# A key tile's split, a modulation row's low part and a layer norm's statistics moved in an adaLN block with linear attention

## The chip, the cores and the metric

The kernel runs on one core of a Trainium2 chip. The metric is the device time of one execution in microseconds (us). TensorE (PE) multiplies, with its weight loads (PEld) overlapping the matmuls; VectorE (DVE), ScalarE (ACT) and GpSimd (POOL) do the elementwise work; the queue of SyncE (SP) issues all the transfers. Each engine runs its instructions strictly in the order in which the program lists them, so moving a line moves work on every engine that it uses.

## The reference

For x of 2048 tokens by 512 features, six rows of 512 come out of `silu(c) @ w_mod`: sa, ca, ga, sb, cb, gb.

```python
h = layernorm(x) * (1 + ca) + sa
q, k, v = split_heads(h @ wqkv)                 # 32 heads of 16
pq, pk = phi(q), phi(k)                         # phi(t) = (t+1 if t>0 else exp(t)) + 1e-6
kv, z = sum_s pk^T v, sum_s pk
x = x + ga * (((pq @ kv) / (pq . z + 1e-6)) @ wo)
h = layernorm(x) * (1 + cb) + sb
x = x + gb * (((h @ w_gate) * (h @ w_up)) @ w_down)   # F = 1376
```

All of it is float32. The kernel keeps this precision in the large products by splitting each operand into a rounded high part and a low part, `a = ah + al`, and adding three products: `ah bh + ah bl + al bh`.

## The kernel before

The 2048 tokens are four chunks of four tiles of 128 tokens. Tile `i` is tile `j = i % 4` of chunk `ch = i // 4`. All working tiles of 128 x 512 take their buffers from one pool of 94, in the order in which the program asks for them; PSUM has four accumulator banks (`acc`) and four working banks (`bank`).

**Splits.** `split(src, h, l)` is one ScalarE copy (L194, the high part) and one subtraction on VectorE (L195, the low part), or on GpSimd where `low=nc.gpsimd` is given. `split_raw` takes two fresh buffers and splits a loaded weight or a row. `k_split_x(i)` does the same for key tile i: it splits the normalised tile `norm[ch].n[j]` into xh and xl (L194/L195, or L386/L387 for chunks 2 and 3). `k_split(i)` splits phi(k) into kh and kl (L405/L406).

**The key loop (L565 to L656)**, one iteration for each of the 16 tiles. Iteration i projects key tile i+2 (`proj(i + 2, wk)`), in some iterations a query tile too, prepares the splits of tile i+1 (`k_split_x`, `k_split`), runs phi on the projected tile (`k_phi`, L372, L373 and L376), adds to z (L399) and accumulates x^T phi(k) of tile i on TensorE (`t_tile`, L414 to L416). In between, the next chunks' layer norms are prepared. In iteration j = 2 of chunks 0 and 1 `nx2.stats` and `rstd_of` (GpSimd's power, L263) start the norm of the chunk after the next. In iteration j = 3 (i = 3 for chunk 2, i = 7 for chunk 3) it goes on:

- i = 3: the shift of tiles 0 and 1 (`nmr_of(0, 2)`, VectorE, L267), their normalised tiles (`xhat_blocks`, ScalarE, L279), their transfers out to DRAM (`lift_out`, SP), and only then `k_split_x(4)` and `k_split(4)`. Tiles 2 and 3 follow further down in the same iteration, with transfers back (`lift_in`, L332, four for each tile).
- i = 7: tiles 0 and 1 with their transfers out, the shift of tiles 2 and 3 (`nmr_of(2, 4)`), these tiles and their transfers out, the sixteen transfers back, and then `k_split_x(8)` and `k_split(8)`.

The transfers turn a tile blockwise; `lift_turn` (VectorE, L336) finishes the turn, `lift_row` (ScalarE, L341) applies the modulation, and `lift_parts` (L349, L351, L352) splits the result. These parts are the left operands of the chunk's projections: those of chunk 2 are wanted first by `proj(8, wk)` in iteration 6, those of chunk 3 by `proj(12, wk)` in iteration 10.

`extra` is a table of work that the loop does at the end of certain iterations; its entries 3, 5, 6 and 7 split the four loaded blocks of the value weight into `wv`. `wv` is used after the loop.

**After the loop (L771 to L817)**, in the order of the program: queries 6 and 7; the split of `accs[5]` (the row gb before its sum over partitions) and, through `mod_row` (L183, L189), its row; the products that make the key-value matrix in the bank `kvps` (L788), masked by L796; denominators of chunk 0, each a product of phi(q) with z (`den_p`, L676) and a sum over a head's 16 features (`den_r`, L682), then an addition and a reciprocal for the chunk (`den_b`, L692 and L693); `den_c(i)` (L700) divides a query tile, `ready(i)` divides it and sends it out (`move_out`), `move_in(i)` fetches it back turned. `w_out(a, b)` multiplies the key-value blocks of groups a and b by the output weight, each product in a bank of its own, read out by VectorE with the row ga (L765), and then splits both. `q_b(i)` is the last step of phi on a query tile (L376) and frees the bank of its projection.

**The attention output (L1275 to L1298).** `turn_a(i)` transposes a query tile on TensorE into a bank (L714); `y_a` is the product that gives the output tile (L838), `y_b` reads it out on ScalarE with the two sums that the second layer norm wants (L250, L251). `norm2[0].rstd_of()` makes the variance of chunk 0 (L260, VectorE) and takes the power on GpSimd (L263); `ln2_nx(0)` is `nmr_of` (L267) and the four normalised tiles (`ln2_xhat`, L272, ScalarE); `ln2_turn` transposes them (L293).

Of the kernel before, what the change touches and what calls it, by code (L numbers as in the profile page):

```python
# [24 lines left out]
def tile_adaln_block(  # L25
# [12 lines left out]
    nc = tc.nc  # L38
# [6 lines left out]
    NCH = S // CH  # L45
# [87 lines left out]
    raw_v = load_qkv(2)  # L133
# [59 lines left out]
    def split(src, h, l, low=None):  # L193
        nc.scalar.activation(h, src, AF.Copy)  # L194
        (low or nc.vector).tensor_tensor(l, src, f32(h), op=ALU.subtract)  # L195

    def split_raw(raw, shape=(P, D), low=None):
        h = B("w", shape, F32R)
        l = B("w", shape, F32R)
        split(raw, h[:raw.shape[0]], l[:raw.shape[0]], low)  # L200
        return h, l
# [158 lines left out]
    def proj(i, w, of=bank):  # L360

        ch, j = divmod(i, NJ)
        ps = of()
        rows = w is wq and i not in FLIPPED
        product(ps.rearrange("p (s q i) -> p s q i", q=NQ, i=BL) if rows else ps,
                [(cut(norm[ch].t[k], j * P, (j + 1) * P), tuple(by_row(x) for x in w[k]) if rows else w[k])
                 for k in range(KD)])
        return ps
# [9 lines left out]
    def k_split_x(i):  # L378
        ch, j = divmod(i, NJ)
        kx[i] = [B("xh", dt=F32R), B("xl", dt=F32R)]  # L380
        if ch not in LIFTED:
            split(norm[ch].n[j], *kx[i])
            return
        x = by_row(norm[ch].n[j])
        h, l = (t.rearrange("p (s q i) -> p s q i", q=NQ, i=BL) for t in kx[i])
        nc.scalar.activation(h, x, AF.Copy)  # L386
        nc.vector.tensor_tensor(l, x, f32(h), op=ALU.subtract)  # L387
# [30 lines left out]
    def q_a(i, ps):  # L418
        phq[i] = B("h")
        q_ps[i] = ps  # L420
        phi_a(ps, phq[i])

    def q_b(i):
        phi_b(q_ps.pop(i), phq[i])
# [113 lines left out]
    accs = {}  # L538
# [6 lines left out]
    def mod_part(v, *ks):  # L545
        if 0 in ks:
            accs[v] = B("f")
        mod_acc(accs[v], raw_m[v], ks)

    extra = {3: lambda: (wv.extend(split_raw(r) for r in raw_v[0:1]),),  # L550
             5: lambda: (wv.extend(split_raw(r) for r in raw_v[1:2]),),
             6: lambda: (wv.extend(split_raw(r) for r in raw_v[2:3]), mod_load(2),),
             7: lambda: (wv.extend(split_raw(r) for r in raw_v[3:4]),),
             8: lambda: (mod_part(2, 0, 1), mod_load(3)),
# [10 lines left out]
    for i in range(NT):  # L565
        ch, j = divmod(i, NJ)
        done = 0
        up = ch + 1 if 0 < ch < NCH - 1 else None
        if i in (6, 10):
            qps = proj(q_at[i], wq)  # L570
        if i > 2 and i != NT - 2:
            ahead[i + 2] = proj(i + 2, wk) if i + 2 < NT else proj(i + 6 - NT, wq)
        if i in q_at and i not in (6, 10):
            qps = proj(q_at[i], wq)
        def turn_x():
            to, *ks = turn_at[i]
            nx.transpose(*ks)
            nx.modulated(ca, sa, *ks, cast=nc.vector)
            norm[to:] = [nx]

        if i == 2:
            turn_x()
            wq.extend(split_blocks(r) for r in raw_q)
        if ch + 2 < NCH and j == 3:
            nx = nx2
            if ch == 0:
                nx.nmr_of(0, 2)
            nx.xhat_blocks(0, 1)
            lifts = [lift_out(f"first_{ch}_{n}", nx.n[n]) for n in range(2)]
            if ch:  # L590
                nx.nmr_of(2, 4)
                nx.xhat_blocks(2, 3)
                lifts += [lift_out(f"first_{ch}_{n}", nx.n[n]) for n in (2, 3)]
                lifts = [lift_in(x) for x in lifts]
        if 0 < i < NT - 1:
            k_split_x(i + 1)
            k_split(i + 1)
        if up and j == 1:
            if up == 2:
                lift_turn(2, lifts[2])  # L600
                lift_turn(3, lifts[3])
            for k in range(KD):
                nx.t[k] = lift_parts(k, lift_row(k, ca, sa))
            norm[up:] = [nx]
        if i in turn_at and i != 2:
            t_tile(i, 0, 1)
            done = 2
            turn_x()
        if i == 2:
            t_tile(i, *range(KD))  # L610
            done = KD
            ahead[i + 2] = proj(i + 2, wk)
        if ch + 2 < NCH and j == 2:
            nx2 = Norm(xts[ch + 2])
            nx2.stats(0, 1)
            nx2.rstd_of(0, 2)
            if ch:
                nx2.stats(2, 3)
                nx2.nmr_of(0, 2)
                nx2.rstd_of(2, 4)  # L620
        if ch == 0 and j == 3:
            nx.stats(2, 3)
            nx.rstd_of(2, 4)
        if i + 2 < NT:
            k_phi(i + 2, ahead.pop(i + 2))
        elif i == NT - 1:
            q_a(i + 6 - NT, ahead.pop(i + 2))
            q_b(i + 6 - NT)
        if i in q_at:
            q_a(q_at[i], qps)  # L630
            q_b(q_at[i])
        if ch == 0 and j == 3:
            nx.nmr_of(2, 4)
            nx.xhat_blocks(2, 3)
            lifts[0], lifts[1] = lift_in(lifts[0]), lift_in(lifts[1])
            lifts += [lift_out(f"first_{ch}_{n}", nx.n[n]) for n in (2, 3)]
            lifts[2], lifts[3] = lift_in(lifts[2]), lift_in(lifts[3])
        if i + 1 < NT:
            z_add(i + 1)
        if i == NT - 2:  # L640
            pairs["z"] = split_raw(zacc, low=nc.gpsimd)
        if i == NT - 1:
            zps = row_sum(pairs["z"])
            zb = consts.tile([P, D], F32, name="zb")
            nc.scalar.activation(zb, zps, AF.Identity, bias=eps_z)
            zq = B("z")
            nc.gpsimd.tensor_copy(zq.rearrange("p (q s i) -> p q s i", q=NQ, i=BL), by_block(zb))
        t_tile(i, *range(done, KD))
        if up == 2 and j == 0 or ch == 1 and j == 3:
            lift_turn(0, lifts[0])  # L650
            lift_turn(1, lifts[1])
        if up == 3 and j == 0:
            lift_turn(2, lifts[2])
            lift_turn(3, lifts[3])
        if i in extra:
            extra[i]()  # L656
# [16 lines left out]
    def den_p(ch, *js, on=None):  # L673
        for j in js:
            pzs[ch, j] = B("f")
            (on or nc.gpsimd).tensor_tensor(pzs[ch, j], phq[ch * NJ + j], zq if ch * NJ + j in FLIPPED else zb, op=ALU.mult)  # L676
# [7 lines left out]
    def den_a(ch, *js, on=None):  # L684

        for j in js:
            den_p(ch, j, on=on)
            den_r(ch, j)

    def den_b(ch, a=0, b=NJ):  # L690
        d = dens[ch][:, a:b]
        nc.vector.tensor_tensor(d, d, (den0q if ch * NJ + a in FLIPPED else den0).unsqueeze(1).to_broadcast([P, b - a, NH]), op=ALU.add)  # L692
        nc.vector.reciprocal(d, d)  # L693

    def den_c(*tiles):

        for i in tiles:
            ch, j = divmod(i, NJ)
            p3 = phq[i].rearrange("p (h i) -> p h i", i=DH)
            nc.vector.scalar_tensor_tensor(p3, p3, EPS_PHI, dens[ch][:, j].unsqueeze(2).to_broadcast([P, NH, DH]),  # L700
                                           op0=ALU.add, op1=ALU.mult)
# [35 lines left out]
    def move_in(*tiles):  # L737

        for i in tiles:
            moved[i] = lift_in(moved[i])  # L740
# [12 lines left out]
    def ready(*tiles):  # L753
        den_c(*tiles)
        move_out(*tiles)
# [3 lines left out]
    def w_out(*gs):  # L759
        fs = []  # L760
        for g in gs:
            ps = bank()
            product(ps, [(cut(kvp, g * P, (g + 1) * P), wo_s[g])])
            f = B("n")
            nc.vector.tensor_tensor(f, ps, ga, op=ALU.mult)  # L765
            fs.append(f)
        for f in fs:
            wp.append((B("w", dt=F32R), B("w", dt=F32R)))
            split(f, *wp[-1])
# [9 lines left out]
    for f in fs:  # L779
        tt.append((B("w", dt=F32R), B("w", dt=F32R)))  # L780
        split(f, *tt[-1])
    q_a(6, ps)
    q_tile(7)
    pairs[5] = split_raw(accs[5], low=nc.gpsimd)
    kvps = bank()
    for g in range(KD):
        a, b = g * P, (g + 1) * P
# [16 lines left out]
    q_a(8, ps)  # L804
    ps = proj(9, wq)
    q_b(8)
    w_out(0, 1)
    q_a(9, ps)
    den_c(0)
    ready(2)  # L810
    move_in(2)
    w_out(2, 3)
    ready(3)
    den_c(1)
    move_in(3)
    q_b(9)
    q_tile(10)  # L817


# [132 lines left out]
    def ln2_xhat(ch):  # L952
        norm2[ch].xhat(0, 1, 2, 3)

    def ln2_nx(ch):
        norm2[ch].nmr_of()
        ln2_xhat(ch)
# [328 lines left out]
    y_step(2, lambda: split_gu(f0, nc.gpsimd))  # L1286
    den_a(1, 1, on=nc.vector)
    y_step(3, lambda: scale_down(f0), turn=False, seed=False)
    den_a(1, 2, 3, on=nc.vector)
    den_b(1)  # L1290
    ps12 = proj(12, wq)
    y_b(3)
    norm2[0].rstd_of()
    ready(4)
    q_a(12, ps12)
    ps13 = proj(13, wq)
    ready(5)
    ln2_nx(0)  # L1298
    q_b(12)
    ready(6)  # L1300
    move_in(4)
# [227 lines left out]
```

## Time and profile before

| | |
|---|---|
| median of 3 runs | 550.17 us (549.89 to 550.17) |
| the profiled execution | 550.99 us, of it 549.3 us from the first to the last instruction |
| mean granted TensorE clock | 0.996 |
| PE busy | 542.7 us (99%) |
| PEld busy | 444.3 us (81%) |
| DVE, ACT, POOL busy | 382.7, 293.1 and 206.4 us |

Times in the profile count from the first instruction of the profiled execution. A row of the timeline reads: start, duration, engine, line of the kernel, operation, output tile and input tiles, output and input shape, count, and in brackets the engine's idle time just before it with what ended that. Engines are pipelined: the next independent instruction may start some 0.1 us before the last one's end. A name like `h` stands for all tiles of that name.

### The profile page before, as it was taken

How to read it: one execution, taken by the hardware profiler on the slowest of the kernel's cores; microseconds unless marked ns; L12 is line 12 of the kernel's file. 1: busy time of each engine (PE TensorE's matmuls, PEld its weight loads, DVE VectorE, ACT ScalarE, POOL GpSimd, SP SyncE). 2: the span in 40 equal slices, each digit the busy share in tenths (PEclk: the TensorE clock that was granted, in tenths of full speed). 3: DMA queues.
4: the chain of work that ended last, by engine and by line, in shares of the span. 5: the costliest groups of instructions: out<-in, count | busy, mean ns of one | idle time of the engine just before them, and what ended most of it. 6: DMA issues, size and time to landing. Idle time of an engine off the chain costs nothing.

```text
span 549.3 us, 7400 instructions
## 1 busy us (share of the span) xinstructions
PE 542.7 (99%) x2432; PEld 444.3 (81%) x2432; DVE 382.7 (70%) x631; ACT 293.1 (53%) x541; POOL 206.4 (38%) x208
## 2 busy tenths in 40 slices
PE   8999999999999999999999999999999999999997
PEld 6888778888878878878888888877888888888886
DVE  6897789989988888769766676985444344434434
ACT  3595777747477774577674545444443444444110
POOL 2001010001003320066696566766666646446100
PEclk9899999999999999999999999999999999999999
DMA  8902426220074245945454061790444122200004
GB/s 281 384 24 78 153 83 216 89 74 2 20 211 143 93 169 159 304 142 152 133 144 124 23 208 39 254 288 16 121 135 114 57 58 58 58 19 1 0 1 154
DMA packets 68455, 65.65 MB, mean 120 GB/s; under 512 B 8448, under 2 KB 46592, under 8 KB 68416
## 3 DMA queue, kind: packets, MB, share of 16 engines
q1 hardware_dynamic: 68416, 65.17, 37.9%
q8 instruction: 19, 0.31, 0.2%
q14 instruction: 20, 0.16, 0.1%
HBM read 46.27 MB, written 18.87 MB: 119 GB/s over the span
## 4 chain that ended last, share of the span: by engine, by line
PE 94%; DVE 2%; ACT 1%; DMA 1%; SPq 1%; issue 0%; POOL 0%; DVEq 0%; POOLq 0%
PE bank L1097 33%; PE acc L1177 6%; PE acc L1178 6%; PE acc L1179 6%; PE acc L838 5%; PE bank L209 5%; PE bank L207 5%; PE bank L208 4%; PE acc L416 3%; PE acc L414 3%; PE acc L415 3%; PE bank L921 2%; PE bank L923 2%; PE bank L922 2%; PE acc L948 1%; PE acc L947 1%
## 5 line engine op out<-in xcount | busy, mean ns | idle before, releaser
L1097 PE MATMUL bank<-h,w 128*128 128x512 f32 (+1 forms) x798 | 184.7, 390 | 0.0
L1097 PEld LDWEIGHTS bank<-h,w 128*128 128x128 f32 (+1 forms) x798 | 148.5, 186 | 33.2 <-ACT bank L1102 0.6
L1102 ACT ACTIVATE bank<-bank 128x512 f32<-128x512 f32 (+1 forms) x38 | 22.2, 583 | 139.5 <-PE bank L1097 139.4
L908 DVE TENSOR_TENSOR x<-acc,x 128x512 f32<-128x512 f32 (+1 forms) x73 | 48.8, 682 | 49.6 <-PE acc L1179 47.9
L1083 POOL TENSOR_TENSOR w<-raw,w 128x256 fp32r<-128x256 f32 (+3 forms) x38 | 40.8, 1073 | 91.2 <-ACT w L1076 91.2
L1177 PE MATMUL acc<-w,kh 128*128 128x512 f32 (+2 forms) x154 | 59.7, 387 | 0.0
L1178 PE MATMUL acc<-w,kh 128*128 128x512 f32 (+2 forms) x154 | 59.6, 387 | 0.0
L1179 PE MATMUL acc<-w,kl 128*128 128x512 f32 (+2 forms) x154 | 59.6, 387 | 0.0
L195 POOL TENSOR_TENSOR w<-raw,w 128x512 fp32r<-128x512 f32 (+1 forms) x26 | 36.7, 1415 | 56.4 <-ACT w L194 52.2
L263 POOL TENSOR_TENSOR rstd<-ve,half 128x2 f32<-128x2 f32 (+3 forms) x13 | 12.6, 970 | 113.0 <-DVE ve L262 67.4
L1083 POOL TENSOR_TENSOR w<-t,w 128x512 fp32r<-128x512 f32 (+1 forms) x38 | 49.2, 1314 | 0.0
L195 DVE TENSOR_TENSOR kl<-u,kh 128x512 fp32r<-128x512 f32 (+1 forms) x38 | 26.4, 735 | 30.6 <-ACT kh L194 30.6
L207 PE MATMUL bank<-w,h 128*128 128x512 f32 x104 | 40.9, 394 | 0.0
L209 PE MATMUL bank<-w,h 128*128 128x512 f32 x104 | 40.9, 393 | 0.0
L208 PE MATMUL bank<-w,h 128*128 128x512 f32 x104 | 40.6, 390 | 0.0
L838 PE MATMUL acc<-w,xh 128*128 128x512 f32 x120 | 37.1, 391 | 0.0
L1156 DVE TENSOR_TENSOR u<-bank,u 128x512 f32<-128x512 f32 (+1 forms) x19 | 13.1, 691 | 31.4 <-PE bank L1097 23.8
L1177 PEld LDWEIGHTS acc<-w,kh 128*128 128x128 f32 (+1 forms) x154 | 28.9, 188 | 6.0
L1179 PEld LDWEIGHTS acc<-w,kl 128*128 128x128 f32 (+1 forms) x154 | 28.9, 188 | 5.9
L1178 PEld LDWEIGHTS acc<-w,kh 128*128 128x128 f32 (+1 forms) x154 | 29.0, 188 | 5.9
L1065 POOL TENSOR_TENSOR t<-raw,t 128x256 f32<-128x256 f32 (+1 forms) x34 | 25.8, 760 | 1.3
L838 PEld LDWEIGHTS acc<-w,xh 128*128 128x128 f32 x120 | 22.5, 188 | 4.6
(215 smaller groups left out, 1114.1 us busy)
## 6 DMA issues: line engine op xcount, KB each, us to landing
raw<-in_w_mod_dram SPq DMA_DIRECT2D x24, 256.0 KB, 3.6
raw<-in_B_w_down_dram SPq DMA_DIRECT2D x20, 256.0 KB, 2.8
raw<-in_B_w_gate_dram SPq DMA_DIRECT2D x36, 128.0 KB, 3.3
raw<-in_B_w_up_dram SPq DMA_DIRECT2D x36, 128.0 KB, 3.5
x<-in_A_x_dram SPq DMA_DIRECT2D x16, 256.0 KB, 5.5
out_dram<-x SPq DMA_DIRECT2D x15, 256.0 KB, 2.7
moved<-h SPq DMA_DIRECT2D x14, 256.0 KB, 2.1
u<-moved SPq DMA_DIRECT2D x56, 64.0 KB, 2.0
```

The costliest lines, as they stand in the source:

```text
L195: (low or nc.vector).tensor_tensor(l, src, f32(h), op=ALU.subtract)
L207: nc.tensor.matmul(ps, ah, bh, start=i == 0, stop=False)
L208: nc.tensor.matmul(ps, ah, bl, start=False, stop=False)
L209: nc.tensor.matmul(ps, al, bh, start=False, stop=i == n - 1)
L838: nc.tensor.matmul(yps[i], x, y, start=False, stop=k == KD - 1 and x is al, skip_group_check=True)
L908: nc.vector.tensor_tensor(xt[:, a:b], dn[j][:, a:b], xt[:, a:b], op=ALU.add)
L1065: sub = lambda out, x, y: (on or nc.gpsimd).tensor_tensor(out, x, y, op=ALU.subtract)
L1083: sub = lambda out, x, y: (on or nc.gpsimd).tensor_tensor(out, x, f32(y), op=ALU.subtract)
L1097: mm = lambda x, y, **kw: nc.tensor.matmul(ps, x[:, k], y, skip_group_check=True, **kw)
L1177: nc.tensor.matmul(ps, hh[:, a:b], dh[:n, c:d], start=i == 0, stop=False)
L1178: nc.tensor.matmul(ps, hh[:, a:b], dl[:n, c:d], start=False, stop=False)
L1179: nc.tensor.matmul(ps, hl[:, a:b], dh[:n, c:d], start=False, stop=i == len(hs) - 1)
```

## The change

Three groups of lines move; nothing else is added or removed.

1. In the key loop at j = 3 of chunks 0 and 1, `k_split_x(i + 1)` comes ahead of the next normalised tiles (at i = 3 after the shift of tiles 0 and 1, at i = 7 ahead of everything of this block). At i = 3 the split of the first block of the value weight comes right behind it and leaves the table `extra`.
2. After the loop the split of `accs[5]` goes ahead of `q_a(6)`, with its low part on VectorE instead of GpSimd; the divisions of tiles 0 and 2 and tile 2's transfers go ahead of `w_out(0, 1)`; `den_c(1)` and `q_b(9)` go ahead of `ready(3)`.
3. In the attention output, `rstd_of` of the second norm goes ahead of the last sum of chunk 1's denominators and their addition and reciprocal, `nmr_of` right behind these, and the normalised tiles right behind `q_a(12)`.

```diff
-    extra = {3: lambda: (wv.extend(split_raw(r) for r in raw_v[0:1]),),
-             5: lambda: (wv.extend(split_raw(r) for r in raw_v[1:2]),),
+    extra = {5: lambda: (wv.extend(split_raw(r) for r in raw_v[1:2]),),
...
             nx = nx2
             if ch == 0:
                 nx.nmr_of(0, 2)
+            k_split_x(i + 1)
+            if ch == 0:
+                wv.append(split_raw(raw_v[0]))
             nx.xhat_blocks(0, 1)
...
         if 0 < i < NT - 1:
-            k_split_x(i + 1)
+            if ch + 2 == NCH or j < 3:
+                k_split_x(i + 1)
             k_split(i + 1)
...
+    pairs[5] = split_raw(accs[5])
     q_a(6, ps)
     q_tile(7)
-    pairs[5] = split_raw(accs[5], low=nc.gpsimd)
...
     q_b(8)
-    w_out(0, 1)
-    q_a(9, ps)
     den_c(0)
     ready(2)
     move_in(2)
+    w_out(0, 1)
+    q_a(9, ps)
     w_out(2, 3)
+    den_c(1)
+    q_b(9)
     ready(3)
-    den_c(1)
     move_in(3)
-    q_b(9)
     q_tile(10)
...
-    den_a(1, 2, 3, on=nc.vector)
-    den_b(1)
+    den_a(1, 2, on=nc.vector)
+    den_p(1, 3, on=nc.vector)
     ps12 = proj(12, wq)
     y_b(3)
     norm2[0].rstd_of()
+    den_r(1, 3)
+    den_b(1)
+    norm2[0].nmr_of()
     ready(4)
     q_a(12, ps12)
+    ln2_xhat(0)
     ps13 = proj(13, wq)
     ready(5)
-    ln2_nx(0)
     q_b(12)
```

## The prediction

> **What bounds the kernel now.** I read the chain of waits first, then the waits of the weight loads, then the timeline around each edit. The chain:
>
> ```profile
> PE 94%; DVE 2%; ACT 1%; DMA 1%; SPq 1%; issue 0%; POOL 0%; DVEq 0%; POOLq 0%
> ```
>
> TensorE is the bound nearly throughout, so an edit can pay only where TensorE stops. Its stops show as waits of its weight loads (microseconds in total, times, longest):
>
> ```profile
> PEld bank L209 <- DVE h L352: 1.0, 3, 0.4
> PEld bank L714 <- DVE h L376: 0.7, 1, 0.7
> ...
> PEld bank L293 <- ACT n L272: 0.6, 1, 0.6
> ```
>
> Row 1 is the key projection of tile 8, which waits for the second chunk's turned tiles (the split at L352); row 2 is the turning of tile 1 (L714); the last is the second layer norm of chunk 0. The edits lie ahead of these three places, and all that can be won is some 2.5 us of 549.3.
>
> **The first edit, at tile 3.** ScalarE idles ahead of the normalised tiles, then does the split of key tile 4 (xh) behind them; the split of the value weight (w) comes an iteration later:
>
> ```profile
> 47.23 1.52 ACT L279 ACTIVATE n<-x,nmr,rstd 128x512 f32<-128x512 f32 x2 [3.97 <-DVE nmr L267]
> 48.66 0.62 ACT L194 ACTIVATE xh<-n 128x512 fp32r<-128x512 f32 x1
> ...
> 55.16 0.61 ACT L194 ACTIVATE w<-raw 128x512 fp32r<-128x512 f32 x1
> 55.68 0.62 ACT L194 ACTIVATE xh<-n 128x512 fp32r<-128x512 f32 x1
> ...
> 64.17 0.81 ACT L341 ACTIVATE f<-wide,col,col 128x512 f32<-128x512 f32 x1 [3.83 <-DVE wide L336]
> ```
>
> Both instructions move into the idle 3.97 us, where they cost nothing; left of the chain, each frees 0.52 us (55.16 to 55.68), 1.04 together. Their VectorE halves (0.61 each, from the two starts below) fall into VectorE's own gap, since at this place the norm's shift (nmr) stays ahead of them:
>
> ```profile
> 49.31 0.69 DVE L195 TENSOR_TENSOR xl<-n,xh 128x512 fp32r<-128x512 f32 x1 [2.11 <-ACT xh L194]
> 49.92 0.69 DVE L406 SCALAR_TENSOR_TENSOR kl<-phi,kh 128x512 fp32r<-128x512 f32 x1
> ...
> 59.24 0.69 DVE L376 SCALAR_TENSOR_TENSOR h<-bank,h 128x512 f32<-128x512 f32 x1 [0.46 <-ACT h L373]
> ```
>
> At 59.24 VectorE waits for ScalarE, and from there on it is busy without a gap up to the row at 64.17; so the turned rows and their splits come 1.04 earlier. The transfers of tiles 2 and 3 on SP's queue follow their tiles, about 0.5 earlier, and still land before VectorE wants them. What TensorE loses there:
>
> ```profile
> 63.80 0.39 PE L207 MATMUL bank<-w,h 128*128 128x512 f32 x1
> ...
> 66.52 0.39 PE L207 MATMUL bank<-w,h 128*128 128x512 f32 x1
> ...
> 70.02 0.39 PE L414 MATMUL acc<-kh,xh 128*128 128x512 f32 x1
> ```
>
> Twelve matmuls take 2.72 us unhindered and 3.50 in tile 8's projection: 0.78 lost, all of it covered by 1.04. **Gain 0.78**; between 0 (if something else of that chain does not move) and 0.78.
>
> **The same edit at tile 7.** Here the split of key tile 8 goes ahead of the shift for tiles 2 and 3 as well, on VectorE's queue:
>
> ```profile
> 77.44 0.68 DVE L399 TENSOR_TENSOR z<-z,phi 128x512 f32<-128x512 f32 x1
> ...
> 80.91 0.69 DVE L387 TENSOR_TENSOR xl<-n,xh 128x512 fp32r<-128x512 f32 x1 [2.11 <-ACT xh L386]
> ...
> 86.05 0.71 DVE L336 STREAM_TRANSPOSE wide<-u 128x512 f32<-128x512 f32 x1 [0.32 <-DMA u<-first]
> ...
> 96.03 0.69 DVE L352 TENSOR_TENSOR h<-f,h 128x512 fp32r<-128x512 f32 x1
> ```
> ```profile
> 78.84 1.52 ACT L279 ACTIVATE n<-x,nmr,rstd 128x512 f32<-128x512 f32 x2 [1.10 <-DVE nmr L267]
> ```
>
> Queued behind the 0.60 of xl are the shift, ScalarE's two tiles at 78.84, their two transfers out on SP and, behind them on SP, all sixteen transfers back. The turn at 86.05 waits for one of those; from it to the last split at 96.03 VectorE has no gap. All this comes 0.60 later by its own clock. TensorE loads that split with next to no slack (96.72 is its end):
>
> ```profile
> 96.80 0.19 PEld L209 LDWEIGHTS bank<-w,h 128*128 128x128 f32 x1
> ```
>
> But VectorE arrives 1.04 earlier and TensorE only 0.78, so of the 0.60 some 0.26 is absorbed and 0.08 is slack: the load is about 0.3 late. A late load costs less than its lateness, since loads run one matmul ahead (0.23): about 0.12 less. **Loss 0.18**; bounds 0 and 0.40 (if nothing is absorbed).
>
> **The row's low part.** GpSimd's subtraction goes to VectorE, into the wait of 0.93 in the first row here (it needs 0.60). It is gone from beside the denominator product of the second row, which took 1.79 next to it; operations of this size take 0.69:
>
> ```profile
> 134.24 0.69 DVE L376 SCALAR_TENSOR_TENSOR h<-bank,h 128x512 f32<-128x512 f32 x1 [0.93 <-ACT h L373]
> 134.85 1.79 DVE L676 TENSOR_TENSOR f<-h,zb 128x512 f32<-128x512 f32 x1
> ...
> 144.92 1.37 DVE L765 TENSOR_TENSOR n<-bank,row 128x512 f32<-128x512 f32 x2 [0.40 <-PE bank L209]
> 146.31 1.38 DVE L195 TENSOR_TENSOR w<-n,w 128x512 fp32r<-128x512 f32 x2
> 147.60 1.29 DVE L700 SCALAR_TENSOR_TENSOR h<-h,den 128x512 f32<-128x512 f32 x2
> 148.80 1.28 DVE L765 TENSOR_TENSOR n<-bank,row 128x512 f32<-128x512 f32 x2
> ```
>
> VectorE gains 1.1 us there but then waits for the key-value product and for ScalarE's copy behind the modulation row: **0**, bounds 0 and 0.4 (the idle at 144.92).
>
> **The new order of the output weights.** The two divisions (L700) go ahead of the first two output-weight products. Without them the products of groups 2 and 3 leave PSUM 0.5 earlier than 148.80, and q_b(9) runs before the third division. What TensorE loses to these two now:
>
> ```profile
> 149.25 0.39 PE L209 MATMUL bank<-w,h 128*128 128x512 f32 x1
> 149.54 0.65 PE L714 MATMUL bank<-ident,h 128*128 128x128 f32 x4
> 150.14 0.50 PE L207 MATMUL bank<-w,h 128*128 128x512 f32 x1
> ...
> 152.76 0.39 PE L209 MATMUL bank<-w,h 128*128 128x512 f32 x1
> 153.40 0.66 PE L714 MATMUL bank<-ident,h 128*128 128x128 f32 x4 [0.25 <-DVE h L376]
> 153.82 0.47 PE L838 MATMUL acc<-w,xh 128*128 128x512 f32 x1
> ```
>
> Unhindered it is 0.23 (2.72 / 12) to the first and 0.42 for four (153.40 to 153.82). So 0.06 + 0.18 at the first place, 0.64 - 0.23 = 0.41 at the second: **gain 0.65**. What is late instead: group 0 is read out of PSUM 0.80 later (144.92 loses its idle 0.40 and gets 1.20 put ahead), ending at 146.41. Four banks, one held by tile 9 until q_b(9): the other three rotate: the transposes at 149.54 start as the read of group 2 ends (148.80 + 0.69), the projection at 150.14 as that of group 3 does. So group 3 takes group 0's bank, and its load stands at
>
> ```profile
> 145.85 0.19 PEld L207 LDWEIGHTS bank<-w,xh 128*128 128x128 f32 x1
> ```
>
> It will be 0.55 late: **loss 0.43**; bounds 0 (another bank) and 0.55. Tile 2's transfers leave SP three us earlier, into an idle queue.
>
> **The second layer norm.** The variance (L260) goes ahead of the last denominator sum, their addition and the reciprocal:
>
> ```profile
> 167.02 0.69 DVE L682 TENSOR_REDUCE den<-f 128x32 f32<-128x512 f32 x1
> ...
> 168.94 0.10 DVE L260 TENSOR_SCALAR ve<-sums 128x4 f32<-128x4 f32 x1
> 169.06 1.29 DVE L700 SCALAR_TENSOR_TENSOR h<-h,den 128x512 f32<-128x512 f32 x2
> 170.65 0.16 DVE L267 SCALAR_TENSOR_TENSOR nmr<-sums,rstd 128x4 f32<-128x4 f32 x1 [0.30 <-POOL rstd L263]
> ```
> ```profile
> 172.99 0.49 PE L293 MATMUL bank<-ident,n 128*128 128x128 f32 x3
> 173.84 0.77 PE L293 MATMUL bank<-ident,n 128*128 128x128 f32 x5 [0.35 <-ACT n L272]
> ```
>
> From variance to shift it takes 1.71 us, of which GpSimd's power is most. Started at 167.02, the power ends at 168.7 beside the sum, the addition and the reciprocal (together 167.12 to 169.04), so the shift comes at 169.04, 1.6 earlier, and with it ScalarE's four tiles. The fourth transposition, due at 172.99 + 3 x 0.11 = 173.32, waits till 173.84: **gain 0.52**, with over a us to spare; bounds 0 and 0.6. The divisions behind (L700) start where they did.
>
> A rule speaks against this. The power now runs beside an addition of two operands in SBUF. The Trainium skill (SBUF — State Buffer, "Who interferes with whom") says that such an instruction and a GpSimd one that reads SBUF lock each other out for the whole instruction; by it, as an estimate, the addition stands till the power ends and the shift comes some 0.8 later, still ahead of need by 0.4: the sum stays. The trace has two divisions with such operands beside the same power, and they ran at 1.29 for both, unhindered; it bears the rule out at 134.85 only.
>
> **The sum.** 0.78 - 0.18 + 0 + 0.65 - 0.43 + 0.52 = 1.34 us. The profiled execution took 550.99 with a span of 549.3, so its successor's span would be 548.0. Against the median of the runs, 550.17, which is 0.82 below that execution: **548.8**.
>
> **The rivals.**
> *Both new losses stay hidden* (tile 8's low part finds VectorE free; group 3 gets a free bank). For it: the split at 96.03 was on time by 0.08 with nothing absorbed. Against: VectorE's queue is in order, and the first product's read cannot start before the divisions. 1.34 + 0.61 = 1.95, 548.2. Chance 0.2.
> *Buffers.* The two new tiles at tile 7 take buffers that the normalised tiles had. If the first is still read by the sum at 77.44 (to 78.12), ScalarE's queue stands till then and the fourth normalised tile starts at 78.12 + 0.52 + 3 x 0.72 = 80.8, not 79.56: 1.24 later instead of 0.60. Loss 0.82 instead of 0.18: 549.5. For it: few buffers are free here; against: no wait of the kind at 76 now. Chance 0.18.
> *The norm's gain goes elsewhere*, the power or the reciprocal being slower side by side: 549.3. Against: the spare us. Chance 0.1.
> *Slower.* The third chunk's turned tiles become the bound: if the last transfers back land late by D at tile 7, tile 12's projection loses D - 0.42, against 1.52 won elsewhere, so it decides from D = 1.94. With D = 2.5 it is 550.7. For it: sixteen transfers in a row on SP's queue behind the moved tiles. Against: by the rows D is 0.60, with the buffers 1.24. Chance 0.07.
>
> **How the numbers follow.** Forecast 0.45, the rest as given. 548.8 is the likeliest; 547.9 to 549.9 takes in the hidden losses, the buffers and the bounds. This kernel's times tell 0.2% (1.1 us, below 549.07) from no change: faster holds the first rival and eight or nine tenths of the forecast, 0.60; slower 0.07; within, the rest, 0.33.
>
> **What would show it.** Tile 8's projection in 2.7 us instead of 3.5; the row of L352 for it without waits; a new wait of L209 on L352 in tile 12's projection; a new wait of group 3's load on L765, none of the two turns; no wait of L293 on the normalised tiles; L676 at 0.68 near 134. The forecast is wrong if tile 8 still waits, or if tile 12's projection or group 3 loses more than 0.5.

## The result, and the profile after

| | before | changed |
|---|---|---|
| median | 550.31 us (549.89 to 551.54, 6 runs) | 548.59 us (548.24 to 549.44, 6 runs) |
| span of the profiled execution | 549.3 us | 546.9 us |
| mean granted TensorE clock there | 0.996 | 1.000 |

The ratio is 0.9967, 95% interval 0.9954 to 0.998. The forecast was 548.8.

The chain of waits and the waits of the weight loads (total, times, longest) of the changed kernel:

```profile
PE 96%; DMA 2%; DVE 1%; ACT 0%; issue 0%; SPq 0%
```
```profile
PEld bank L207 <- DVE n L768: 0.5, 1, 0.5
...
PEld bank L209 <- DVE h L352: 0.4, 1, 0.4
```

Two kinds of row are gone, L293 for the normalised tiles and L714 (now L717) for the query tiles. The row of L209 has one wait where it had three, and it is another one, in tile 12. The row of L207 was there before with 0.2, behind the first turn; it is another wait now, that of group 3's load.

To see what each stop is worth, take the same matmul by its count in both executions (both have 2432) and subtract its starts. What this difference changes by across a stretch, in us, minus for time won:

```
            start   tile8  tile12  group3   turns   norm2    ffn1    rest    all
after       -0.77   -0.78   +0.26   +0.36   -0.77   -0.58   -0.06   -0.07   -2.41
```

("turns" are the transpositions of query tiles 0 and 1; "norm2" the transpositions of the second layer norm and what stands around them, 172 to 176 us of before; "ffn1" from there to 221 us.) All but the first of these columns lie behind an edit of the change. The first does not: nothing is changed ahead of 40 us. Most of it comes out of these matmuls, of before and of after (start, duration, ... count):

```profile
16.26 2.03 PE L486 MATMUL acc<-w,h 128*128 128x512 f32 x4
18.09 1.06 PE L486 MATMUL bank<-w,h 128*128 128x512 f32 x2
```
```profile
16.42 1.18 PE L486 MATMUL acc<-w,h 128*128 128x512 f32 x4
17.44 0.63 PE L486 MATMUL bank<-w,h 128*128 128x512 f32 x2
```

The profiled execution of before ran four such matmuls in 2.03 us, that of after in 1.18. The traces show why: between 16 and 20 us the granted clock of TensorE was 0.57 in before and 1.00 in after. The same stretch shows 0.59 and 0.61 in e2_tile7 and e12_first, and there this column is -0.33 and -0.28; in all other versions it shows 1.00, and the column lies between -0.77 and -1.39. So the column belongs to the execution, not to the kernel, and the profiled spans (2.4 us apart) overstate the change. Without it the traces differ by 1.64 us, the medians by 1.72. Medians have this stretch of low clock in them too: beside the experiments the kernel before ran 71 times, 31 of them with a mean granted clock below 0.999, and on each of the three chips these took 0.8 to 0.9 us more in the median than the others.

**Tile 8.** ScalarE, then its turned row, then TensorE in the changed kernel:

```profile
42.38 0.62 ACT L194 ACTIVATE xh<-n 128x512 fp32r<-128x512 f32 x1
42.90 0.61 ACT L194 ACTIVATE w<-raw 128x512 fp32r<-128x512 f32 x1
46.45 1.52 ACT L279 ACTIVATE n<-x,nmr,rstd 128x512 f32<-128x512 f32 x2 [2.94 <-DVE nmr L267]
...
62.35 0.82 ACT L341 ACTIVATE f<-wide,col,col 128x512 f32<-128x512 f32 x1 [3.82 <-DVE wide L336]
```
```profile
63.01 0.39 PE L207 MATMUL bank<-w,h 128*128 128x512 f32 x1
...
65.50 0.39 PE L209 MATMUL bank<-w,h 128*128 128x512 f32 x1
```

Both copies lie in the idle time ahead of the normalised tiles; the idle left is 2.94 us where it was 3.97. The first turned row comes at 62.35, 1.82 earlier, of which 0.77 is the start: 1.05 for the edit. The twelve matmuls go from 63.01 to 65.50 + 0.23, 2.72 us, without a wait.

**Tile 12.** VectorE and the one late weight load:

```profile
76.82 0.69 DVE L387 TENSOR_TENSOR xl<-n,xh 128x512 fp32r<-128x512 f32 x1
77.42 0.16 DVE L267 SCALAR_TENSOR_TENSOR nmr<-mv,rstd 128x2 f32<-128x2 f32 x1
...
84.84 0.71 DVE L336 STREAM_TRANSPOSE wide<-u 128x512 f32<-128x512 f32 x1 [0.84 <-DMA u<-first]
...
94.81 0.69 DVE L352 TENSOR_TENSOR h<-f,h 128x512 fp32r<-128x512 f32 x1
```
```profile
95.56 0.19 PEld L209 LDWEIGHTS bank<-w,h 128*128 128x128 f32 x1 [0.39 <-DVE h L352]
```

The split (xl) stands ahead of the shift (nmr); the turn at 84.84 waits 0.84 for a transfer back, where it waited 0.32.

**After the loop.** The product at 133.52 takes 0.68 where it took 1.79, and VectorE then waits for TensorE: the row's low part is free. Then the two output-weight products and group 3's load, and TensorE's turns:

```profile
133.52 0.68 DVE L679 TENSOR_TENSOR f<-h,zb 128x512 f32<-128x512 f32 x1
...
136.93 0.69 DVE L799 TENSOR_TENSOR n<-bank,mask 128x512 f32<-128x512 f32 x1 [0.69 <-PE bank L209]
...
144.25 1.28 DVE L768 TENSOR_TENSOR n<-bank,row 128x512 f32<-128x512 f32 x2
```
```profile
144.99 0.19 PEld L207 LDWEIGHTS bank<-w,xh 128*128 128x128 f32 x1 [0.50 <-DVE n L768]
```
```profile
148.52 0.60 PE L717 MATMUL bank<-ident,h 128*128 128x128 f32 x4
148.88 0.48 PE L207 MATMUL bank<-w,h 128*128 128x512 f32 x1
...
151.73 0.60 PE L717 MATMUL bank<-ident,h 128*128 128x128 f32 x4
152.09 0.71 PE L841 MATMUL acc<-w,xh 128*128 128x512 f32 x2
```

**The second layer norm**, VectorE and GpSimd:

```profile
165.59 0.16 DVE L260 TENSOR_SCALAR ve<-sums 128x4 f32<-128x4 f32 x1
165.70 0.69 DVE L685 TENSOR_REDUCE den<-f 128x32 f32<-128x512 f32 x1
166.42 0.29 DVE L695 TENSOR_TENSOR den<-den,den0q 128x128 f32<-128x128 f32 x1
166.75 0.95 DVE L696 RECIPROCAL den<-den 128x128 f32<-128x128 f32 x1
167.62 0.10 DVE L267 SCALAR_TENSOR_TENSOR nmr<-sums,rstd 128x4 f32<-128x4 f32 x1
```
```profile
165.89 1.01 POOL L263 TENSOR_TENSOR rstd<-ve,half 128x4 f32<-128x4 f32 x1 [0.77 <-DVE ve L260]
```

The power lies beside the sum, the addition and the reciprocal; the addition (166.42) takes 0.29 beside it, as it took without it before. The shift follows at 167.62 without a wait.

### The profile page after: what moved, and what is told of

Read it like the earlier page. It is cut to its first block, busy times and chain, and to the rows that moved or that the text cites. A ratio compares the mean times of both kernels' runs of the same rounds, so it can differ in the third digit from the quotient of the medians.

```text
span 546.9 us, 7392 instructions
## 1 busy us (share of the span) xinstructions
PE 540.3 (99%) x2432; PEld 442.6 (81%) x2432; DVE 381.9 (70%) x632; ACT 293.3 (54%) x541; POOL 204.4 (37%) x207
## 4 chain that ended last, share of the span: by engine, by line
PE 96%; DMA 2%; DVE 1%; ACT 0%; issue 0%; SPq 0%
PE bank L1100 33%; PE acc L841 7%; PE acc L1181 6%; PE acc L1180 6%; PE acc L1182 6%; PE bank L207 4%; PE bank L209 4%; PE bank L208 4%; PE acc L416 3%; PE acc L414 3%; PE acc L415 3%; PE bank L924 2%; PE bank L926 2%; PE bank L925 2%; DMA raw<-in_w_mod_dram 1%; PE acc L951 1%
## 5 line engine op out<-in xcount | busy, mean ns | idle before, releaser
L207 PE MATMUL bank<-w,h 128*128 128x512 f32 x104 | 40.8, 392 | 0.0
L209 PE MATMUL bank<-w,h 128*128 128x512 f32 x104 | 40.7, 391 | 0.0
```

Of the source, the lines that this page charges most:

```text
L207: nc.tensor.matmul(ps, ah, bh, start=i == 0, stop=False)
L209: nc.tensor.matmul(ps, al, bh, start=False, stop=i == n - 1)
```

## The experiments

All medians are beside runs of the kernel before on the same chip. The table has what the profiles of all versions show, by the same subtraction as above:

```
            start   tile8  tile12  group3   turns   norm2    ffn1    rest    all
e1_tile3    -1.00   -0.78   +0.00   +0.00   -0.01   +0.13   -0.05   -0.08   -1.78
e9_key      -0.89   -0.54   +0.02   +0.00   -0.01   +0.33   +0.16   -0.02   -0.94
e2_tile7    -0.33   -0.02   +0.56   +0.00   -0.00   +0.25   +0.14   +0.02   +0.61
e3_order    -1.39   -0.02   +0.00   +0.41   -0.76   +0.96   +0.32   +0.00   -0.46
e4_norm     -0.98   -0.02   +0.02   +0.00   -0.01   -0.58   -0.02   +0.36   -1.22
e5_no7      -1.27   -0.78   +0.00   +0.36   -0.76   -0.58   -0.05   +0.01   -3.08
e6_group    -1.09   -0.78   +0.28   -0.00   -0.77   -0.05   +0.76   -0.01   -1.65
e7_both     -1.08   -0.78   +0.02   +0.00   -0.77   -0.05   +0.73   -0.06   -1.99
e8_pool     -1.29   -0.78   +0.60   +0.36   -0.77   -0.58   +0.10   -0.03   -2.39
e10_scale   -1.18   -0.78   +0.00   -0.00   -0.77   -0.58   +1.25   -0.07   -2.12
e11_best    -1.14   -0.78   +0.00   +0.36   -0.76   -0.58   +0.94   -0.00   -1.96
e12_first   -0.28   -0.78   +0.45   +0.00   -0.77   -0.58   +0.11   -0.02   -1.86
```

### The parts alone

**e1_tile3**: the kernel before with the edit at tile 3 alone.

```diff
-    extra = {3: lambda: (wv.extend(split_raw(r) for r in raw_v[0:1]),),
-             5: lambda: (wv.extend(split_raw(r) for r in raw_v[1:2]),),
+    extra = {5: lambda: (wv.extend(split_raw(r) for r in raw_v[1:2]),),
...
                 nx.nmr_of(0, 2)
+                k_split_x(i + 1)
+                wv.append(split_raw(raw_v[0]))
...
-            k_split_x(i + 1)
+            if i != 3:
+                k_split_x(i + 1)
```

> The kernel before with the first edit at tile 3 alone (split of key tile 4 and of the first value block ahead of the normalised tiles of chunk 2; at tile 7 the old order). Theory 'the stops add': the projection of tile 8 takes 2.7 us instead of 3.5, tile 12's has no wait, all else as before; 0.8 us off the kernel before, 549.5 for 550.3. Rival 'start of the kernel' (the gain is a different course of the clock in the first 20 us): tile 8's projection still 3.5, time as before.

Measured: 549.21 against 550.55 us, ratio 0.9973 (0.9962 to 0.9984). Tile 8's stop is gone (-0.78), and tile 12 loses nothing. The medians show more than that, 1.34, because all eight runs of this kernel had a mean clock of 0.999 or more; against the 17 such runs of the kernel before (550.02) it is 0.81.

**e9_key**: the same, but the value weight's split stays where it was.

```diff
                 nx.nmr_of(0, 2)
+                k_split_x(i + 1)
...
-            k_split_x(i + 1)
+            if i != 3:
+                k_split_x(i + 1)
```

> The kernel before with key tile 4's split alone moved ahead of the normalised tiles at tile 3; the split of the value weight stays at the end of that iteration. If the two splits free 0.52 us each on ScalarE, the turned tiles come 0.52 earlier and tile 8's projection, which lost 0.78, still waits some 0.25: a gain of 0.5 to 0.6, ratio 0.999. Rival: the order alone matters and not the instruction taken out of the chain, then the whole 0.78 is gained and no wait is left (ratio 0.9985); or the key's split gives nothing by itself, since ScalarE's copy is waited for in either place, then 0.

Measured: 549.89 against 550.72 us, ratio 0.9986 (0.9975 to 0.9996). Tile 8 wins 0.54, and a late load is left in its projection:

```profile
68.25 0.19 PEld L209 LDWEIGHTS bank<-w,h 128*128 128x128 f32 x1 [0.39 <-DVE h L352]
```

One copy of 0.52 us taken out of ScalarE's chain is worth 0.54 here, and two use the stop up (e1_tile3); so the step "1.04 freed covers 0.78 lost" holds in its working, not only in its sum.

**e2_tile7**: the kernel before with the edit at tile 7 alone.

```diff
                 nx.nmr_of(0, 2)
+            if ch:
+                k_split_x(i + 1)
             nx.xhat_blocks(0, 1)
...
-            k_split_x(i + 1)
+            if i != 7:
+                k_split_x(i + 1)
```

> The kernel before with the first edit at tile 7 alone. Theory 'the stops add', with the absorption that the prediction claims: without tile 3's edit VectorE does not come 0.26 earlier than TensorE, so the last split for tile 12's projection is 0.5 late and that projection loses about 0.4 us instead of 0.2; 0.4 slower, 550.7 for 550.3. Rival 'the loss is a matter of buffers, not of VectorE's queue': the loss is the same 0.2 as in the changed kernel, and the normalised tiles start late.

Measured: 550.96 against 550.55 us, ratio 1.0007 (0.9997 to 1.0017). Tile 12 loses 0.56. VectorE's turn and the last load:

```profile
86.44 0.71 DVE L336 STREAM_TRANSPOSE wide<-u 128x512 f32<-128x512 f32 x1 [0.97 <-DMA u<-first]
```
```profile
97.16 0.19 PEld L209 LDWEIGHTS bank<-w,h 128*128 128x128 f32 x1 [0.50 <-DVE h L352]
```

The prediction's upper bound was 0.40, the rival's loss 0.2. VectorE's split is not where it goes: by then VectorE idles 0.97 for a transfer back. The lateness reaches the turn over the transfers: against TensorE, the one that the turn waits for is issued 0.57 us later than in before and lands 0.68 later.

**e3_order**: the kernel before with the order of the divisions and output-weight products alone.

```diff
     q_b(8)
-    w_out(0, 1)
-    q_a(9, ps)
     den_c(0)
     ready(2)
     move_in(2)
+    w_out(0, 1)
+    q_a(9, ps)
     w_out(2, 3)
+    den_c(1)
+    q_b(9)
     ready(3)
-    den_c(1)
     move_in(3)
-    q_b(9)
```

> The kernel before with the new order of divisions and output-weight products alone, the row's low part left on GpSimd. Theory: TensorE stops 0.4 us before group 3's product (bank of group 0), and neither before the turn of tile 0 nor that of tile 1 (0.7 won); 0.3 off, 550.0. Rival 'the row's low part pays for it': with GpSimd's subtraction in place VectorE is later and the stop before group 3 grows to 0.8, or the turns still stop; no gain or a loss.

Measured: 550.27 against 550.55 us, ratio 0.9995 (0.9983 to 1.0006). Group 3 loses 0.41 and the turns win 0.76, as in the whole change; but then the second norm takes back 0.96 in the profiled execution. Its view of VectorE and of TensorE:

```profile
162.18 0.69 DVE L888 TENSOR_TENSOR raw<-raw,row 128x512 f32<-128x512 f32 x1 [0.41 <-DMA raw<-in_B_w_down_dram]
```
```profile
172.41 0.33 PE L293 MATMUL bank<-ident,n 128*128 128x128 f32 x1 [0.38 <-ACT n L272]
173.11 0.77 PE L293 MATMUL bank<-ident,n 128*128 128x128 f32 x5 [0.38 <-ACT n L272]
```

TensorE reaches the norm 1.69 earlier than in before, start included. VectorE reaches the product of the first down weight with the row gb (`scale_down`, L888, 162.91 in before) only 0.73 earlier; behind it on VectorE stand the last denominators and the norm. 1.69 - 0.73 is the 0.96. It has two parts. The sum ahead of the product starts 1.22 earlier (161.08 for 162.30), so VectorE's chain gains 0.47 less than TensorE. The other 0.49 is the wait for the weight's load: the product follows that sum after 1.10 us, in before after 0.61.

The second part is not shown to be the work of this edit. The load's time from issue to landing varies by itself: 3.65 us in before and 5.18 in e4_norm, whose kernel is the same up to there, 5.76 here. In e1_tile3, e9_key and e2_tile7 the product is 0.11, 0.31 and 0.19 late by the same wait, and that is nearly all of their 0.13, 0.33 and 0.25 in the column norm2. The profiled execution of e3_order (550.55 us) was also among the longer ones: its nine runs at a mean clock of 0.999 or more have a median of 549.98, those of the kernel before 550.02. So the new order pays nothing by itself, and pays where the norm is out of the way, as part 3 puts it.

**e4_norm**: the kernel before with part 3 alone (the last hunk of the diff above).

> The kernel before with the second layer norm's statistics moved alone. Theory: no wait of the transposes L293 on the normalised tiles, the shift 1.6 us earlier, 0.55 us off, 549.75. Rival 'VectorE is late next' (the divisions and the splits behind wait instead): the stop comes back within the next 30 us and the gain is under 0.2.

Measured: 549.79 against 550.55 us, ratio 0.9985 (0.9975 to 0.9996). The norm's stop goes (-0.58) and nothing comes in its place near it. So the rival, which had the stop come back within 30 us, is out. The +0.36 in the last column is one weight load far behind (L1097, at 361.58), which waits 0.82 for VectorE where it waited 0.41 in before; why is open.

### Parts taken out of the whole

**e5_no7**: the changed kernel with key tile 8's split left in its old place.

```diff
-            k_split_x(i + 1)
             if ch == 0:
+                k_split_x(i + 1)
                 wv.append(split_raw(raw_v[0]))
...
-            if ch + 2 == NCH or j < 3:
+            if i != 3:
                 k_split_x(i + 1)
```

> The changed kernel with tile 7's part of the first edit undone. Theory 'the stops add': tile 12's projection loses nothing (2.72 us instead of 2.95), 0.23 us better than the changed kernel, about 548.4 for its 548.6. Rival: some other queue needs the early split of tile 8, and the time is that of the changed kernel or worse.

Measured: 548.12 against 550.38 us, ratio 0.9959 (0.9946 to 0.9972); tile 12 loses nothing, the rest is as in the whole. The same turn in this kernel:

```profile
83.80 0.71 DVE L336 STREAM_TRANSPOSE wide<-u 128x512 f32<-128x512 f32 x1 [0.37 <-DMA u<-first]
```

**e8_pool**: the changed kernel with the row's low part on GpSimd again.

```diff
-    pairs[5] = split_raw(accs[5])
+    pairs[5] = split_raw(accs[5], low=nc.gpsimd)
```

> The changed kernel with the row's low part on GpSimd again (the split stays where the change put it). Theory: VectorE's first denominator product takes 1.8 us beside it instead of 0.7, and VectorE waits for the key-value product less, but no stop of TensorE changes: the time of the changed kernel, 548.6. Rival: the stop before group 3 grows by 0.4.

Measured: 548.55 against 550.38 us, ratio 0.9961 (0.9949 to 0.9974), not to be told from the whole, and group 3 loses 0.36 as there, so the rival's 0.4 more did not come. Its tile 12 loses 0.60, with the same code there as the changed kernel, whose profile shows 0.26.

### Freeing group 3's bank

**e6_group** and **e7_both**: the changed kernel, and e5_no7, with tile 2's division put behind the reads of groups 2 and 3, so that group 0's bank comes free earlier; tile 2's transfers follow it. The edit, the same in both:

```diff
+    den_c(0)
     w_out(0, 1)
     q_a(9, ps)
-    den_c(0)
-    ready(2)
+    w_out(2, 3, between=lambda: ready(2))
     move_in(2)
-    w_out(2, 3)
```

(read against the kernel before; `between` runs after the products' reads and ahead of their low parts)

> The changed kernel with the division of tile 2 moved behind the reads of groups 2 and 3 (the division of tile 0 alone stays ahead of groups 0 and 1). Theory: group 0 is read 0.6 earlier, group 3 finds its bank free, the turns stay without a stop: 0.36 us better than the changed kernel, 548.25. Rival 'tile 2 becomes late': its transfers leave 4 us later, the turn of tile 2 waits for them and TensorE stops at the output product of tile 2: no gain or a loss.

> Both: tile 7's part undone and tile 2's division behind the reads. Theory 'the stops add': 0.6 us better than the changed kernel, 548.0; 2.2 to 2.3 us better than the kernel before. Rival: the two gains overlap, 548.3.

Measured: 549.36 (ratio 0.9979, 0.997 to 0.9989) and 549.22 us (0.9978, 0.9968 to 0.9988) against 550.38. Group 3's stop is gone, so its cause is the bank; yet both take longer than what they were made from, since norm2 wins only 0.05 and ffn1 loses 0.76 and 0.73. The rival of e6_group had the loss, but not the place: TensorE does not stop at tile 2's output product. The views of VectorE, GpSimd and the weight loads of e7_both:

```profile
161.86 1.20 DVE L892 TENSOR_TENSOR raw<-raw,row 128x512 f32<-128x512 f32 x1 [1.10 <-DMA raw<-in_B_w_down_dram]
162.98 1.78 DVE L679 TENSOR_TENSOR f<-h,z 128x512 f32<-128x512 f32 x1
...
178.56 1.68 DVE L316 TENSOR_TENSOR h<-f,h 128x512 fp32r<-128x512 f32 x1
```
```profile
178.41 2.98 POOL L195 TENSOR_TENSOR w<-raw,w 128x512 fp32r<-128x512 f32 x2 [4.09 <-issue]
```
```profile
180.29 0.19 PEld L926 LDWEIGHTS bank<-h,w 128*128 128x128 f32 x1 [0.79 <-DVE h L316]
```

Tile 2's transfers now leave SP later, and queued behind them there are the loads of the feed-forward weights. The down weight's load is issued 0.69 us later than in e5_no7, counted from the same matmul ahead of group 3, and part of its lateness is again the time that it takes to land (5.35 us here, 4.62 there). VectorE waits 1.10 us for it, and everything behind, the norm and then the low parts of the normalised rows (L316), comes later. At 178.56 the last of these meets two splits on GpSimd that began 0.15 before it, and takes 1.68 instead of 0.69. In e5_no7 it comes ahead of them and takes 0.69:

```profile
177.43 0.69 DVE L316 TENSOR_TENSOR h<-f,h 128x512 fp32r<-128x512 f32 x1
```
```profile
178.08 2.56 POOL L195 TENSOR_TENSOR w<-raw,w 128x512 fp32r<-128x512 f32 x2 [4.90 <-issue]
```

Three kernels test this reading. **e10_scale** is e7_both, and **e11_best** e5_no7, with the product moved out of the way of the norm; **e12_first** is e7_both with its load issued first of the three.

```diff
-    y_step(3, lambda: scale_down(f0), turn=False, seed=False)
+    y_step(3, turn=False, seed=False)
...
     q_b(12)
+    scale_down(f0)
```
```diff
     def load_ffn(f):
         f0, n = fts[f]
+        if not raw_f:
+            d = load(w_down[f0:f0 + n, :], "raw")
+            raw_f[f] = (load(wg_v[:, :, f0:f0 + n], "raw"), load(wu_v[:, :, f0:f0 + n], "raw"), d)
+            return
```

> The version with group 3's bank freed early and without the part at tile 7 (549.22, ratio 0.9978), with the product of the down weight and the row moved behind q_b(12), out of VectorE's queue ahead of the second norm. If that product's wait for its load is what gave 0.5 back at the second norm and 0.8 near 180 us, both go: L293 waits for no normalised tile and the ratio falls to 0.995 to 0.9957 (547.8 to 548.1). Rival: the later transfers of tiles 2 and 3 act through something else (ScalarE's split of the up weight, the turned queries); then the norm still comes late and the ratio stays at 0.997 to 0.998.

> The changed kernel without its part at tile 7 (548.12, ratio 0.9959), with the same product moved behind q_b(12). In that kernel the product did not wait for its load and the normalised tiles were in time, so 0.6 us more of VectorE's time ahead of the norm buys nothing: ratio 0.9955 to 0.9963, about 548.1. Rival: the load's landing is so near that it costs in part of the executions; then the median falls by 0.2 to 0.4 and the runs spread less. Other rival: the product now late delays the down weight's split and loses up to 0.6 near 180 us.

> The same version as the second of this call (group 3's bank freed early), but instead of moving the product its load is issued first of the three of that block, about 1 us earlier. If the landing is the cause, the product does not wait, and the ratio falls from 0.9978 to about 0.995 to 0.996. Rival: the up weight, now last of the three, lands late instead and holds ScalarE's split and, behind it in ScalarE's queue, the sums that the norm wants: then the wait moves to ScalarE and the ratio stays at 0.997 to 0.998.

Measured, against 550.72 us:

| | median | ratio |
|---|---|---|
| e10_scale | 548.69 (548.28 to 549.83, 6 runs) | 0.9963 (0.9951 to 0.9975) |
| e11_best | 549.00 (548.82 to 550.39, 8 runs) | 0.9971 (0.9961 to 0.9981) |
| e12_first | 547.93 (547.54 to 549.18, 5 runs) | 0.9953 (0.9939 to 0.9968) |

e12_first is as its theory has it: no wait for the load, no second norm late, and the low part clear of GpSimd.

```profile
161.95 0.68 DVE L896 TENSOR_TENSOR raw<-raw,row 128x512 f32<-128x512 f32 x1
162.54 0.68 DVE L679 TENSOR_TENSOR f<-h,z 128x512 f32<-128x512 f32 x1
...
179.01 0.69 DVE L316 TENSOR_TENSOR h<-f,h 128x512 fp32r<-128x512 f32 x1
```
```profile
179.16 2.95 POOL L195 TENSOR_TENSOR w<-raw,w 128x512 fp32r<-128x512 f32 x2 [4.40 <-ACT w L194]
```

The up weight now lands last, and the rival that expected it to hold the norm over ScalarE was wrong: norm2 wins its whole 0.58.

e10_scale is right in its half: the norm is on time (-0.58), so the product's wait was what held it. But the ratio it expected did not come, and e11_best, expected to change nothing, lost. In both, the moved product and its 0.60 stand ahead of the low parts now, and the last of them meets GpSimd after its start. In e10_scale, and then in e11_best:

```profile
178.24 1.60 DVE L316 TENSOR_TENSOR h<-f,h 128x512 fp32r<-128x512 f32 x1
```
```profile
177.78 3.21 POOL L195 TENSOR_TENSOR w<-raw,w 128x512 fp32r<-128x512 f32 x2 [5.11 <-issue]
```

```profile
178.45 1.60 DVE L316 TENSOR_TENSOR h<-f,h 128x512 fp32r<-128x512 f32 x1
```
```profile
178.21 2.99 POOL L195 TENSOR_TENSOR w<-raw,w 128x512 fp32r<-128x512 f32 x2 [5.32 <-issue]
```

The column ffn1 shows 1.25 and 0.94 lost. By the starts of the matmuls 0.66 of each is lost where TensorE waits 0.8 us for this low part (0.65 and 0.64 in e6_group and e7_both). In e10_scale 0.24 more goes at two earlier low parts. The other 0.30 and 0.26 lie near 217 us, at splits of turned tiles (L352); what makes these late is not shown. The other rival of e11_best, a late split of the down weight, does not show: what TensorE waits for near 180 us is L316. So the two late losses of e6_group and e7_both are two things: the load's landing at the norm, and the meeting with GpSimd later.

e12_first and e5_no7 have lower medians than the changed kernel, 547.93 and 548.12 against 548.59, but their intervals overlap with its own, so the ratios alone don't set the three apart. At a mean clock of 0.999 or more e5_no7 took 547.91 to 548.12 us (3 runs), the changed kernel 548.24 to 548.60 (4) and e12_first 547.54 to 548.94 (4). They were not run beside each other, so this is a hint that e5_no7 takes less time than the whole, and not more.

## Why the prediction was right, point by point

**Tile 8: right, in mechanism and size.** Said 0.78 won of 1.04 freed; measured 0.78 and 1.05. One copy alone wins 0.54 (e9_key).

**Tile 7: right in place and path, its size and bound off.** Said a loss of 0.18, at most 0.40; the changed kernel's profile shows 0.26, those of e6_group, e2_tile7 and e8_pool with the same edit 0.28, 0.56 and 0.60. The last two even pass the 0.5 which the prediction had named as a sign of being wrong. The term counted one lateness, VectorE's 0.60, passed on without a change through SP and the transfers. In the changed kernel this holds: VectorE's last split ends 2.19 us after the start of tile 12's projection in before, 1.98 in e1_tile3 (0.21 absorbed, said 0.26) and 2.57 in the changed kernel (0.59 more). But the turn of the tile waits for a transfer back (0.32 before, 0.84 and 0.97 with the edit), so what ends last is a landing, and landings vary. In e8_pool the last of the four turns waits too (0.25), for a transfer that lands 0.48 later against TensorE than in the changed kernel. What varies them stays open: e12_first, without this edit, lost 0.45 in its profiled execution, again behind a turn that waited for a transfer, while the eight other profiles without it lost at most 0.02. That transfer took 2.40 us from issue to landing there, 1.93 in before. The turn and the last load of e12_first:

```profile
85.20 0.71 DVE L336 STREAM_TRANSPOSE wide<-u 128x512 f32<-128x512 f32 x1 [0.79 <-DMA u<-first]
```
```profile
96.25 0.19 PEld L209 LDWEIGHTS bank<-w,h 128*128 128x128 f32 x1 [0.50 <-DVE h L352]
```

That the edit is a loss is shown by the profiles: all four with it lose 0.26 to 0.60, eight of the nine without it nothing; in the medians, 548.59 and 548.12, it is 0.47 us, with ratios whose intervals overlap.

**The buffers at tile 7: did not happen.** That rival wanted the fourth normalised tile late behind a buffer; ScalarE's tiles in the changed kernel wait for the shift alone and follow each other at once:

```profile
77.62 1.52 ACT L279 ACTIVATE n<-x,nmr,rstd 128x512 f32<-128x512 f32 x2 [1.70 <-DVE nmr L267]
79.04 0.71 ACT L405 ACTIVATE kh<-phi,eps_phi 128x512 fp32r<-128x512 f32 x1
```

**The row's low part: right at 0.** The denominator product fell from 1.79 to 0.68 and VectorE then waited for TensorE, as the step said; with the low part back on GpSimd the time is the same (e8_pool).

**The output weights: right, two sizes slightly off.** The turns won 0.77 (said 0.65): the step took 0.42 for four unhindered transpositions, and they take 0.36 (148.52 to 148.88, 151.73 to 152.09), 0.06 less at each of the two places. Group 3 lost 0.36 (said 0.43; its load waited 0.50, said 0.55). That group 3 takes group 0's bank was read from the order of the reads, and e6_group and e7_both show it, since the stop goes with the earlier read. But the step's remark on tile 2's transfers, "into an idle queue", was only half of what they do: the loads that stand behind them on SP move with them, and in e6_group, where these transfers leave later, the second norm pays for it.

**The second norm: right.** Said 0.52, measured 0.58, and in e4_norm the same. The lock that the Trainium skill states (SBUF — State Buffer, "Who interferes with whom") would have stretched the addition to the end of the power; it took 0.29 beside it, so for this small power (four elements in each partition) the rule was not borne out. It was at L316, where an operation of 128x512 on GpSimd stood against one of 128x512: VectorE's took 1.6 to 1.7 us where GpSimd's began first and 0.69 where VectorE's did, which agrees with that section's rule that the one issued first holds the shared ports till its end. In e6_group, e7_both, e10_scale and e11_best VectorE's ended 0.55 us behind the end of GpSimd's first split, whenever it had begun.

**The sum.** Said 1.34; measured 1.64 by the trace without the start, 1.72 by the medians. The difference is the sum of sizes named here (turns 0.12, group 3 0.07, norm 0.06, tile 7 -0.08) and 0.13 in the two last columns. The time itself came out 0.2 below the forecast with some luck: the forecast took off the 0.82 between the profiled execution and the median of three runs, which is the size of the stretch of low clock, and tile 7's term is 0.26 in the one profile and 0.60 in another. That the terms could be added at all was less safe than the prediction made it. Alone, the middle part wins 0.35 ahead of the second norm (0.76 - 0.41) and loses 0.96 there; 0.49 of that is the wait for the down weight, and 0.47 would be left without it, since TensorE comes earlier and VectorE's chain to the norm does so by less. In the whole change the third part has the shift ready in time, so nothing is given back (in e8_pool the product waits 0.41 for its load, as in e3_order, and norm2 wins its 0.58); the prediction had named its reserve of over a us, but not that the term of the output weights depends on it.

## What to carry to other kernels

An edit that frees TensorE in one place makes it arrive earlier at each later one, so a part that wins in its place may win nothing alone (e3_order), and a part that makes room later (here the norm) decides what the earlier ones are worth; test parts in pairs, not only alone. A wait that ends with a landing changes from one execution to the next, so read it in several profiles before putting it down to an edit. When transfers are moved, look at what is queued behind them on the same queue: here a load wanted some 15 us later was worth more than the wait that the move took away. And where a VectorE operation just gets in ahead of a large GpSimd one, a shift of 0.3 us (from 0.15 ahead to 0.15 behind) costs VectorE a whole microsecond, and TensorE 0.65 of it here.

## What the runs showed of the hardware

The split of 128x512 on VectorE (L316, two operands in SBUF) took 0.69 us when it began 0.15 or 0.65 us ahead of GpSimd's split (e12_first, e5_no7), and 1.68 and 1.60 when it began 0.15 or 0.46 behind it (e7_both, e10_scale). The loser is the one that begins second: in before VectorE's began 0.01 ahead (181.07), and GpSimd's took 1.84, the next of GpSimd's 1.30. A power of 128x4 on GpSimd did nothing to VectorE's addition beside it (0.29).

The same early matmuls of the kernel took 2.03 us for four in one execution and 1.18 in another. The granted clock from 16 to 20 us was 0.57 and 1.00 in these two, the mean over the whole 0.996 and 1.000. What decides which of the two an execution gets is open. It makes 0.8 to 0.9 us of the whole time, as much as the effects studied here, so two profiles, or two short lists of runs, can't be compared without the clock.

A load of 256 KB, issued at the same place of the program, took 3.65 us to land in one execution (before) and 5.18 in another (e4_norm); issued first of its three it took 2.67 (e12_first).
